# A gated feed-forward layer behind pooled attention: the last 3072 tokens by seven products of half-size blocks, with combined weights streamed from DRAM

## The chip, the cores and the metric

The kernel runs on one core of a Trainium2 chip. Its engines have a queue each and work in parallel: TensorE (PE in the profile; PEld is its weight load), VectorE (DVE), ScalarE (ACT), GpSimd (POOL), and SyncE (SP), whose queue issues the transfers here. Each queue is worked through in order. The metric is the device time of one execution in microseconds, the median of several runs.

## The reference

Only the arithmetic matters; S is 576, so K and V are averaged over 8 rows to 72 rows.

```python
k_p = k.reshape(B, H, Sp, 8, D).mean(axis=3)        # B = 8 images, H = 8 heads, D = 64
v_p = v.reshape(B, H, Sp, 8, D).mean(axis=3)
scores = (q @ k_p.transpose(0, 1, 3, 2)) / sqrt(D)
attn = exp(scores - max(scores)); attn = attn / (sum(attn) + 1e-9)
x = (attn @ v_p).transpose(0, 2, 1, 3).reshape(4608, 512)
h = x @ w_in                                         # 512 -> 2048
g = h * clip(h + 3, 0, 6) / 6
out = g @ w_out                                      # 2048 -> 512
```

## The kernel before

The 4608 tokens are worked through in blocks, `BLOCKS = [512, 256, 384] + [512] * 6 + [384]`. For a block the kernel has x in transposed form (4 chunks of 128 model dimensions by the block's tokens), as a sum of two reduced-precision parts, `xhi` and `xlo`; the weights lie in SBUF in two such parts as well (`w_in_hi`, `w_in_lo`, `w_out_hi`, `w_out_lo`, made once at the start, in the pool `const`). A product of two such matrices takes three matmuls: high by high, high by low, low by high.

A block runs 16 steps, one for each group f of 128 of the 2048 hidden columns. `Step.h` (matmuls on L782) computes h for f: 4 chunks by 3 matmuls, as wide as the block has tokens. `relu` (ACT, L790) and `gate` (DVE, L794) make g; `hi` (ACT, L798) and `lo` (DVE, L802) split it. `Step.out` (L812), two steps later, adds g for f into one PSUM bank per 128 tokens: 3 matmuls of 512 columns for each. After the last f the banks are scaled (ACT, L818) and stored (L819).

Attention for the next block runs between these matmuls. `Paced` hands its steps out, one or a few at each `slot()`. A block of 384 tokens has three tiles of 128 tokens with two head groups each; for each of these six, `scores` does the products (L412), the maximum (DVE, L416), four exponentials on ACT (L420; each is an ACTIVATE and a read of its sum), the reciprocal (DVE, L436 and L437) and the division on POOL (L448, L454); then transposes on PE (L518, L520), their copies on ACT and DVE, and the products with V (L583), copied into `x` by ACT (L585). `side_steps` load and pool K and V of the next image. `split_x` (L561, L562) splits x before a block's first h.

The start, up to the fourth step of block 1, has an order written out by hand (`ORDER`); after it a scheduler sets each queue's order when the program is built, from data dependences and an estimate of times. On the chip the queues then keep that order.

## Time and profile before

| | |
|---|---|
| median of 3 runs | 921.58 us (921.29 to 921.69) |
| span of the profiled execution, first to last instruction | 920.7 us |
| PE busy in it | 908.4 us, 99% |
| DVE, ACT, POOL busy | 456.5, 461.5, 81.1 us |
| granted TensorE clock | 1.000 |
| transfers | 57.19 MB, mean 62 GB/s |

The profile gives no time of the profiled execution apart from its span; the median of the runs lies 0.9 us above the span, for what surrounds the first and the last instruction. Rows of instructions give line, engine, operation, tiles (out<-in), shapes, count, then busy time and mean ns of one. In the chain of waits, one row is start, duration and what ran. In the timeline, "SPq" is a DMA issue by SP.

### The profile page before, as it was taken

To read this page: it belongs to the slowest core of one execution; us is meant where nothing else is said; L and a number is where in the kernel's file an instruction comes from. 1 tells how busy PE (TensorE), PEld (TensorE's weight loads), DVE (VectorE), ACT (ScalarE), POOL (GpSimd) and SP (SyncE) were. 2 spreads that over 40 slices of the span, in tenths; PEclk is the share of its full clock that TensorE was granted. 3 is DMA by queue.
4 is the path that set the end of the run, shared out by engine and by line. 5 is a ranking of instruction groups with operands and counts; after the bars stand their busy time and mean duration, and the time that the engine had idled before them with its cause. 6 is when DMAs were issued, how large, how long until landed. Compare 5 with 4: busy or idle time off the path is not lost.

```text
span 920.7 us, 12711 instructions
## 1 busy us (share of the span) xinstructions
PE 908.4 (99%) x4568; PEld 777.6 (84%) x4568; DVE 456.5 (50%) x916; ACT 461.5 (50%) x1340; POOL 81.1 (9%) x167
## 2 busy tenths in 40 slices
PE   7899999999999999999999999999999999999998
PEld 6788889999888888888888888888888888888997
DVE  6999855475356333824356326633356224332322
ACT  5998665465355434633456335633545344333322
POOL 4100001021000100101011101110101001000000
PEclk9999999999999999999999999999999999999999
DMA  9970203050031002300042004200210000000100
GB/s 295 391 262 0 92 12 121 1 167 18 1 113 59 24 1 79 106 12 6 0 143 59 12 1 136 60 12 1 91 40 25 1 34 24 1 0 1 47 1 35
DMA packets 41935, 57.19 MB, mean 62 GB/s; under 512 B 7568, under 2 KB 23696, under 8 KB 41872
## 3 DMA queue, kind: packets, MB, share of 16 engines
q1 hardware_dynamic: 41728, 56.37, 19.0%
q8 instruction: 36, 0.59, 0.3%
q14 instruction: 27, 0.22, 0.1%
q10 hardware_dynamic: 144, 0.00, 0.0%
HBM read 46.93 MB, written 9.44 MB: 61 GB/s over the span
## 4 chain that ended last, share of the span: by engine, by line
PE 96%; DMA 3%; DVE 1%; issue 0%; SPq 0%; ACT 0%; ACTq 0%; DVEq 0%
PE pso L812 43%; PE psh L782 43%; PE psa L583 4%; PE psa L412 4%; PE psa L518 2%; DMA raw<-w_in_l 1%; DMA raw<-w_out_l 1%; DMA stage<-k_l 1%; PE psa L520 0%; SPq L257 0%; ACT stage L420 0%; DVE u L689 0%; DVE u L700 0%; DVE stage L448 0%; DVE a L510 0%
## 5 line engine op out<-in xcount | busy, mean ns | idle before, releaser
L782 PE MATMUL psh<-xhi,w 128*128 128x512 f32 (+2 forms) x1288 | 401.9, 372 | 0.0
L812 PE MATMUL pso<-w,ghi 128*128 128x512 f32 (+1 forms) x1184 | 367.0, 391 | 0.0
L782 PEld LDWEIGHTS psh<-xhi,w 128*128 128x128 f32 x1288 | 237.7, 188 | 36.1 <-issue 0.4
L812 PEld LDWEIGHTS pso<-w,ghi 128*128 128x128 f32 x1184 | 214.2, 188 | 36.0
L782 PE MATMUL psh<-xlo,w 128*128 128x512 f32 (+2 forms) x644 | 237.4, 369 | 0.0
L794 DVE SCALAR_TENSOR_TENSOR g<-g,psh 128x512 f32<-128x512 f32 (+2 forms) x161 | 101.3, 629 | 271.5 <-ACT g L790 270.3
L812 PE MATMUL pso<-w,glo 128*128 128x512 f32 (+1 forms) x592 | 225.9, 386 | 0.0
L790 ACT ACTIVATE g<-psh,small 128x512 f32<-128x512 f32 (+2 forms) x161 | 103.7, 644 | 208.7 <-PE psh L782 192.3
L782 PEld LDWEIGHTS psh<-xlo,w 128*128 128x128 f32 x644 | 121.2, 188 | 18.1
L802 DVE TENSOR_TENSOR glo<-g,ghi 128x512 fp32r<-128x512 f32 (+2 forms) x161 | 102.3, 635 | 62.0 <-ACT ghi L798 60.1
L812 PEld LDWEIGHTS pso<-w,glo 128*128 128x128 f32 x592 | 111.1, 188 | 21.7
L798 ACT CAST ghi<-g 128x512 fp32r<-128x512 f32 (+2 forms) x161 | 92.9, 577 | 70.0 <-DVE g L794 67.4
L420 ACT ACTIVATE e<-psa,mx 128x72 f32<-128x72 f32 x256 | 78.6, 322 | 50.6 <-DVE mx L416 49.9
L448 POOL TENSOR_TENSOR a<-e,sm 128x256 f32<-128x256 f32 x60 | 40.5, 675 | 513.5 <-PE pso L812 180.3
L420 ACT ACTIVATION_READ_ACCUMULATOR e<-psa,mx 128x1 f32 x256 | 52.9, 207 | 0.0
L416 DVE TENSOR_REDUCE mx<-psa 128x4 f32<-128x288 f32 x72 | 32.3, 453 | 29.5 <-PE psa L412 29.0
L412 PEld LDWEIGHTS psa<-kbd,qt 128*128 128x128 f32 x288 | 43.1, 189 | 4.2
L412 PE MATMUL psa<-kbd,qt 128*128 128x144 f32 x288 | 45.5, 285 | 0.0
L585 ACT COPY x<-psa 128x192 f32<-128x192 f32 (+7 forms) x60 | 22.9, 386 | 32.6 <-PE psa L583 32.4
L332 DVE TENSOR_REDUCE vsum<-vst 128x64 f32<-128x512 f32 (+1 forms) x36 | 37.7, 1065 | 2.6 <-DMA vst<-v_l 2.0
L436 DVE TENSOR_SCALAR sm<-sm 128x4 f32<-128x4 f32 x72 | 12.6, 178 | 48.9 <-ACT e L420 45.7
L529 ACT CAST ahi<-psa 128x256 fp32r<-128x256 f32 (+1 forms) x70 | 24.5, 352 | 18.7 <-PE psa L518 9.8
(93 smaller groups left out, 630.7 us busy)
## 6 DMA issues: line engine op xcount, KB each, us to landing
out<-o SPq DMA_DIRECT2D x35, 256.0 KB, 2.3
raw<-w_in_l SPq DMA_DIRECT2D x16, 512.0 KB, 8.5
raw<-w_out_l SPq DMA_DIRECT2D x16, 512.0 KB, 9.2
kst<-k_l SPq DMA_DIRECT2D x28, 288.0 KB, 3.0
qt<-q_l SPq DMA_DIRECT2D x28, 256.0 KB, 3.3
vst<-v_l SPq DMA_DIRECT2D x24, 256.0 KB, 3.1
vst<-vr_l SPq DMA_DIRECT2D x36, 64.0 KB, 1.9
stage<-k_l SPq DMA_DIRECT2D x4, 288.0 KB, 4.1
```

Source lines behind the costliest of these rows:

```text
L332: nc.vector.tensor_reduce(out=vs[:n, p], in_=st[:n, : POOL * D].rearrange("p (o d) -> p d o", o=POOL), axis=AX.X, op=ALU.add)
L412: nc.tensor.matmul(to, qt[:, p, :], kbds[b % 2][:, p, :], start=r == 0, stop=r == last)
L416: nc.vector.tensor_reduce(out=self.mx, in_=self.ps, axis=AX.X, op=ALU.max, negate=True)
L420: nc.scalar.activation(self.e[:, h], self.ps[:, h], AF.Exp, bias=self.mx[:, h : h + 1], accum_out=self.sm[:, h : h + 1])
L448: engine.tensor_tensor(out=self.a[:, : 4 * D].rearrange("p (h s) -> p h s", h=4), in0=e[:, :, :D], in1=sm[:, :, None].broadcast_to([P, 4, D]),
L583: nc.tensor.matmul(ps, l, r, start=n == 0, stop=n == len(mms) - 1)
L782: nc.tensor.matmul(self.ps, l[f][:, c, :], r[:, c, :], start=c == 0 and i == 0, stop=c == NCC - 1 and i == 2)
L790: nc.scalar.activation(self.g, self.ps, AF.Relu, bias=half, scale=1.0 / (6.0 * WSCALE))
L794: nc.vector.scalar_tensor_tensor(out=g, in0=g, scalar=1.0, in1=self.ps, op0=ALU.min, op1=ALU.mult)
L798: nc.scalar.copy(self.ghi, self.g)
L802: nc.vector.tensor_tensor(out=self.glo, in0=self.g, in1=self.ghi.bitcast(F32), op=ALU.subtract)
L812: nc.tensor.matmul(pos, l, r[:, cols], start=f == 0 and i == 0, stop=f == NF - 1 and i == 2)
```

## The change

The first 1536 tokens are four blocks of 512, 256, 384 and 384 and run as before (`PLAIN = 4`). The other 3072 form four super blocks of two 384-token halves. In a super block both layers are computed by a 2x2 split of each matrix product, with the seven products of the Strassen-Winograd scheme in place of eight: halves of the tokens, of the contraction, and of the output columns.

For h, the hidden columns are taken in 8 pairs of f; each pair has seven products (`N1`, 56 in all) of a combined weight block (128 hidden columns by 256 model dimensions) and a combined x block (256 dimensions by 384 tokens). Each is 2 chunks by 3 matmuls of 384 columns. `PERIOD` interleaves pairs so that a product has its PSUM bank free. Sums between products are kept by ACT copies (`keep`) and DVE adds (`plus`); four gates per pair leave g in four quadrants, `g_of[i]`, that stay in SBUF. For out, `N2` runs the seven kinds in the order `KINDS`, each over the 8 pairs: a g quadrant or a sum of quadrants (made on POOL) is split by `split_op` on ACT and DVE, and multiplied by a combined w_out block of 256 columns: 3 token tiles by 3 matmuls of 256 columns. The seven combined x blocks (`x_ops`) are made on POOL, ACT and DVE during the last 16 products of the super block before.

The combined weights do not fit in SBUF. They are made during the plain blocks 2 and 3, one `sums_of` call at each of the 32 steps: six POOL operations in a buffer `wq`, a high part on ACT in `wh`, a low part on DVE in place, and eight DMA writes of 64 KB to DRAM; blocks that need no sum are copied from the weights. `wq` and `wh` have two buffers each. In a super block `next_w` loads them back, two products to a 512 KB chunk, into a ring of 6 chunks (`ws`), five ahead; each super block reads all 56 chunks.

SBUF is shared out anew: the pools `early` and `const` are released behind block 3, and `late`, with everything of the super blocks, lies on the same addresses; `x1` lies over the weights of f = 14 and 13. The attention of the next blocks is spread over N1 and over the first 40 products of N2; half of block 3's attention moves into block 1. The last tile's split in two banks at the end of the program is gone.

The diff, cut to its core:

```diff
-BLOCKS = [512, 256, 384] + [512] * 6 + [384]
+BLOCKS = [512, 256, 384, 384] + [384] * 8
+PLAIN = 4
+HALF = 384
...
+PERIOD = ((1, 0), (2, 0), (7, 1), (5, 0), (6, 0), (4, 1), (3, 0))
+KINDS = (1, 2, 6, 5, 7, 3, 4)
+RAW_LEFT = {1: (0, 0), 2: (0, 1), 4: (1, 1)}
+RAW_RIGHT = {1: (0, 0), 2: (1, 0), 3: (1, 1)}
+CHUNK, NSTREAM, AHEAD, NOP, NC, NRO = 2, 6, 5, 4, 4, 4
 WSCALE = 2.0**8
+GSCALE = WSCALE**-2
...
     psum = ctx.enter_context(tc.tile_pool(name="psum", bufs=1, space=PSUM))
+    const = tc.alloc_tile_pool(name="const", bufs=1, reuse_waits="tile")
+    early = [tc.alloc_tile_pool(name="early0", bufs=1, reuse_waits="tile")]
...
+    NPR = NF // 2
+    N1 = [(1, i, o) for t in range(NPR + 1) for o, d in PERIOD for i in [t - d] if 0 <= i < NPR]
+    N2 = [(2, i, o) for o in KINDS for i in range(NPR)]
+    stream = N1 + N2
+    place_of = {x: n for n, x in enumerate(stream)}
...
+    def dram_of(kind, i, o):
+        n = place_of[kind, i, o]
+        return w_dram[n // CHUNK][:, n % CHUNK]
...
+    def sums_of(kind, i, h):
+        half = slice(h * P, (h + 1) * P)
+        qs = early[-1].tile([P, 4, P], F32, name="wq", bufs=2)
+        pairs = [w_of[2 * i + r, kind - 1].bitcast(F32).rearrange("p m (q c) -> p m q c", q=2) for r in range(2)]
+        for r, w in enumerate(pairs):
+            nc.gpsimd.tensor_tensor(
+                out=qs[:, 2 * r : 2 * r + 2], in0=w[:, 0, :, half], in1=w[:, 1, :, half], op=ALU.add
+            )
+        mixed = combine_left(qs, nc.gpsimd) if kind == 1 else combine_right(qs, nc.gpsimd)
+        hi = early[-1].tile([P, 4, P], F32, name="wh", bufs=2)
+        nc.scalar.copy(hi.bitcast(F32R), qs)
+        nc.vector.tensor_tensor(out=qs.bitcast(F32R), in0=qs, in1=hi, op=ALU.subtract)
+        for o, q in mixed.items():
+            for m, t in enumerate((hi, qs)):
+                nc.sync.dma_start(dram_of(kind, i, o)[:, m, half], t[:, q])
+        if h:
+            return
+        for o, (r, q) in (RAW_LEFT if kind == 1 else RAW_RIGHT).items():
+            nc.sync.dma_start(dram_of(kind, i, o), pairs[r][:, :, q])
+    def combine_left(q, engine):
+        def op(to, a, b, how):
+            engine.tensor_tensor(out=q[:, to], in0=q[:, a], in1=q[:, b], op=how)
+        op(0, 0, 2, ALU.subtract)
+        op(2, 2, 3, ALU.add)
+        op(3, 3, 0, ALU.subtract)
+        op(1, 1, 3, ALU.subtract)
+        return {7: 0, 3: 1, 5: 2, 6: 3}
...
+    def next_w(x):
...
+        n, loaded = w_stream
+        while n * CHUNK <= place_of[x] + CHUNK * AHEAD and n < len(w_dram):
+            loaded[n] = late.tile([P, CHUNK, 2, 2 * P], F32R, name="ws", bufs=NSTREAM)
+            nc.sync.dma_start(loaded[n].bitcast(F32), w_dram[n])
+            n += 1
+        w_stream[0] = n
+        at = place_of[x]
+        return loaded[at // CHUNK][:, at % CHUNK]
+    def split_op(t, src):
+        nc.scalar.copy(t[:, 0], src)
+        nc.vector.tensor_tensor(out=t[:, 1], in0=src, in1=t[:, 0].bitcast(F32), op=ALU.subtract)
...
+    def x_ops(j, steps, now=False):
...
+        a, b = (x_tile(i, "x", F32) for i in (j, j + 1))
+        b11, b21, b12, b22 = a[:, :2], a[:, 2:], b[:, :2], b[:, 2:]
+        def split(o, src):
+            def make(c):
+                if c == 0:
+                    x_op[o] = late.tile([P, 2, 2, HALF], F32R, name=f"x{o}")
+                split_op(x_op[o][:, :, c], src[:, c])
+            return [lambda c=c: make(c) for c in range(2)]
...
+        early_ones = split(1, b11) + split(2, b21)
+        late_ones = (
+            mix(None, b22, b12, ALU.subtract)
+            + split(3, b22)
+            + mix(b12, b12, b11, ALU.subtract)
+            + mix(b11, b11, None, ALU.add)
+            + [lambda c=c, o=o: split(o, mid[0])[c]() for o in (7,) for c in range(2)]
+            + split(6, b11)
+            + mix(b21, b21, b11, ALU.subtract)
+            + split(5, b12)
+            + split(4, b21)
+        )
...
+    def super_block(j, first_att, second_att):
...
+        def bank(names, i, n=HALF):
+            return psum.tile([P, DM], F32, name="psx", tag=names[i % len(names)])[:, :n]
+        def gate(src, q):
...
+            nc.scalar.activation(r, src, AF.Relu, bias=half_low, scale=GSCALE / (6.0 * WSCALE))
+            nc.vector.scalar_tensor_tensor(
+                out=g_of[i][:, k], in0=r, scalar=GSCALE, in1=src, op0=ALU.min, op1=ALU.mult
+            )
...
+        def plus(q, ps, kept):
+            i, k = q
+            nc.vector.tensor_tensor(out=g_of[i][:, k], in0=ps, in1=kept, op=ALU.add)
+            gate(g_of[i][:, k], q)
+        def keep(c, ps):
+            nc.scalar.copy(c, ps)
+            return c
...
+        for x in N1:
+            _, i, o = x
+            if o == 1:
+                g_of[i] = late.tile([P, 4, HALF], F32, name=f"g{i}")
+                c = [late.tile([P, 2, HALF], F32, name="c", bufs=NC) for _ in range(2)]
+                chain[i] = [bank(["h0", "h1", "o0"], i), bank(["o1"], i), bank(["o2"], i), c, {}]
+            X, Y, Z, c, kept = chain[i]
+            ps = {1: X, 2: Z, 3: Y, 4: X, 5: Y, 6: X, 7: X}[o]
+            w, t = next_w(x), ops[o]
+            paced.slot()
...
+            if o == 1:
+                kept[1] = keep(c[0][:, 0], X)
+            elif o == 2:
+                plus((i, 0), Z, kept[1])
+            elif o == 5:
+                kept[5] = keep(c[1][:, 0], Y)
+            elif o == 6:
+                kept[2] = keep(c[0][:, 1], X)
+            elif o == 3:
+                plus((i, 2), Y, kept[2])
+            elif o == 7:
+                plus((i, 3), X, kept[5])
+            elif o == 4:
+                gate(X, (i, 1))
+                g = g_of[i]
+                mix_of[i] = late.tile([P, HALF], F32, name=f"e{i}")
+                nc.gpsimd.tensor_tensor(out=g[:, 2], in0=g[:, 2], in1=g[:, 3], op=ALU.add)
+                nc.gpsimd.tensor_tensor(out=mix_of[i], in0=g[:, 2], in1=g[:, 0], op=ALU.subtract)
...
+        paced = Paced(second_att, len(N2) - n_tail)
+        X2, Y2 = ([bank(names, p, 2 * P) for p in range(NT2)] for names in (["o0", "o3", "h0"], ["h1", "o1", "o2"]))
...
+        def result(t, m, ps, kept):
+            o = late.tile([P, 2 * P], F32, name="o", tag="ro", bufs=NRO)
+            if kept is None:
+                nc.scalar.copy(o, ps)
+            else:
+                nc.vector.tensor_tensor(out=o, in0=ps, in1=kept, op=ALU.add)
+            store(t, m, o)
...
+        for n, x in enumerate(N2):
+            _, i, o = x
...
+            t = late.tile([P, 2, HALF], F32R, name="op", bufs=NOP)
+            split_op(t, src)
+            if o == 1:
+                nc.gpsimd.tensor_tensor(out=g[:, 0], in0=g[:, 3], in1=mix_of[i], op=ALU.subtract)
+            elif o == 2:
+                nc.gpsimd.tensor_tensor(out=g[:, 1], in0=g[:, 1], in1=mix_of[i], op=ALU.subtract)
+            w = next_w(x)
+            if n < len(N2) - n_tail:
+                paced.slot()
+            elif ahead:
+                ahead.pop(0)()
...
+            if n == len(N2) - n_tail - 1:
+                paced.upto(len(paced.steps))
+                if j + 2 < len(BLOCKS):
+                    ahead = first_x + later_x
+            if i < NPR - 1:
+                continue
+            if o in (1, 5, 6):
+                c = late.tile([P, 2, HALF], F32, name="c", bufs=NC).rearrange("p a b -> p (a b)")
+                kept[o] = [keep(c[:, p * 2 * P : (p + 1) * 2 * P], ps) for p, ps in enumerate(X2 if o != 5 else Y2)]
...
-            if steps[0].blk.j == 1 and u == 3:
+                if side:
+                    side.pop(0)()
+            if j == 1 and u == 3:
                 window.append(len(traced))
+                paced.add_more()
...
             if u == len(steps) - 1:
-                paced.upto(len(attention))
-                if attention:
-                    split_x(steps[0].blk.j + 1)
-            if u >= len(steps) and steps[0].blk.j == len(BLOCKS) - 1:
-                continue
+                paced.upto(len(paced.steps))
+                if j + 1 < PLAIN and j != 1:
+                    split_x(j + 1)
             if u >= lag:
                 steps[u - lag].out(slot)
...
+        assert not side
+        if j == 1:
+            early.pop().release()
+            early.append(tc.alloc_tile_pool(name="early1", bufs=1, reuse_waits="tile"))
+            split_x(j + 1)
...
+    third = att_steps(3)
+    cut = len(third) // 2
+    for j, mine, more, side in (
+        (1, att_steps(2), third[:cut], ()),
+        (2, third[cut:] + att_steps(4), (), side_weights[:NF]),
+        (3, att_steps(5), (), side_weights[NF:]),
+    ):
         blk = Block(j, ["o0", "o1", "o2", "o3"])
-        run([Step(blk, f, 0, blk.nt) for f in range(NF)], 2, att_steps(j + 1))
+        run([Step(blk, f, 0, blk.nt) for f in range(NF)], 2, mine, more=more, side=side)
+    early.pop().release()
+    const.release()
+    late = ctx.enter_context(tc.tile_pool(name="late", bufs=1, reuse_waits="tile"))
+    supers = range(PLAIN, len(BLOCKS), 2)
+    x_ops(PLAIN, [], now=True)
+    for j in supers:
+        last = j == supers[-1]
+        super_block(j, [] if last else att_steps(j + 2), [] if last else att_steps(j + 3))
```

Three places in the order of the queues. First ACT, at the end of block 1 (tokens 512 to 767), toward block 2. Before, the splits of x for block 2 (`xhi`) stand ahead of eight exponentials (`e`) and the evictions of block 1's sums (`o<-pso`):

```order
L790 ACTIVATE g<-psh,small 128x256
L561 CAST xhi<-x 128x384 x4
L798 CAST ghi<-g 128x256
L420 ACTIVATE e,sm<-psa,mx 128x72 x8
L818 ACTIVATE o<-pso 128x512 x2
L790 ACTIVATE g<-psh,small 128x384
```

After, at the same place:

```order
L809 ACTIVATE g<-psh,small 128x256
L438 ACTIVATE e,sm<-psa,mx 128x72 x4
L817 CAST ghi<-g 128x256
L438 ACTIVATE e,sm<-psa,mx 128x72 x8
L836 ACTIVATE o<-pso 128x512 x2
L585 CAST xhi<-x 128x384 x4
```

The splits of x that block 2's first h needs now stand behind the exponentials and evictions. Next ACT after the change at the end of block 3, from its evictions toward `x_4321`, the first combined x block (`x1`) of the first super block:

```order
L836 ACTIVATE o<-pso 128x512 x3
L609 COPY x<-psa 128x384
L438 ACTIVATE e,sm<-psa,mx 128x72 x12
L900 CAST wh<-wq 128x512
L438 ACTIVATE e,sm<-psa,mx 128x72 x4
L547 CAST ahi<-psa 128x2x128
L438 ACTIVATE e,sm<-psa,mx 128x72 x2
L900 CAST wh<-wq 128x512
L438 ACTIVATE e,sm<-psa,mx 128x72 x2
L547 CAST ahi<-psa 128x2x128
L558 CAST arem<-psa 64x128
L438 ACTIVATE e,sm<-psa,mx 128x72 x2
```

Behind these stand two more exponentials, a copy of each kind (`arem`, `ahi`), and then the splits of `x1`. All 24 exponentials of a block's attention and the high parts of the last two weight sums are between the end of the plain blocks and the first operand of the first super block. Last SP after the change at the same point, where the writes of the last weight sum (`wd<-wh`, `wd<-wq`) stand ahead of the first chunk of streamed weights (`ws<-wd_86`):

```order
L904 DMA wd_125<-wq 128x128
L904 DMA wd_129<-wq 128x128
L904 DMA wd_141<-wh 128x128
L904 DMA wd_141<-wq 128x128
L904 DMA wd_133<-wh 128x128
L904 DMA wd_133<-wq 128x128
L246 DMA vst<-v_l 128x512
L251 DMA vst<-vr_l 32x512
L944 DMA ws<-wd_86 128x1024
L944 DMA ws<-wd_87 128x1024
```

Before, there was no such stream: SP had loads of q, k and v and stores alone here.

## Prediction

> **What bounds the kernel now.** I read the busy shares of the page first, then the chain of waits, then a table by stage.

> ```profile
> PE 908.4 (99%) x4568; PEld 777.6 (84%) x4568; DVE 456.5 (50%) x916; ACT 461.5 (50%) x1340; POOL 81.1 (9%) x167
> PEclk9999999999999999999999999999999999999999
> PE 96%; DMA 3%; DVE 1%; issue 0%; SPq 0%; ACT 0%; ACTq 0%; DVEq 0%
> PE pso L812 43%; PE psh L782 43%; PE psa L583 4%; PE psa L412 4%; PE psa L518 2%; DMA raw<-w_in_l 1%; DMA raw<-w_out_l 1%; DMA stage<-k_l 1%; PE psa L520 0%; SPq L257 0%; ACT stage L420 0%; DVE u L689 0%; DVE u L700 0%; DVE stage L448 0%; D
> 0.00:38.00 38.00, 28.99 (x188) 26.16 (x189) 28.31 (x65) 27.44 (x94) 12.67 (x29) 1.00 1.00 332
> 270.00:860.00 590.00, 590.00 (x2811) 494.31 (x2810) 261.90 (x533) 266.40 (x807) 51.21 (x102) 1.00 0.13 40
> 860.00:920.70 60.70, 57.44 (x329) 53.31 (x327) 14.97 (x28) 15.82 (x29) 0.00 (x0) 1.00 0.04 14
> ```

> PE works for 99% of the span at a granted clock of 1.000, which I take for the changed kernel too. In the long middle it has no gap at all (590.00 of 590.00 us), while DVE works 261.90, ACT 266.40 and POOL 51.21 us, and DMA moves 40 GB/s. The 9.0 us in which PE waits lie in the first 38 us, which the change leaves almost as they are, and the 3.3 us of the last row. So PE's matmuls are the time: fewer or narrower matmuls shorten it directly, unless they let PE wait. What a matmul costs stands in the chain, by width:

> ```profile
> 271.50 2.72 PE pso L812 x12
> 862.87 2.11 PE psh L782 x12
> 145.31 1.42 PE psh L782 x12
> 497.51 2.75 PE psh L782 x12
> ```

> From 2.72, 2.11 and 1.42 us for twelve, one of 512 columns takes 0.227, of 384 0.176, of 256 0.118 us. Most rows of the chain with twelve of 512 read as the one at 497.51, 0.229; I use 0.228, 0.1755 and 0.119. Check: 3012 of 512 columns, 384 of 384 and 312 of 256 in the lines 782 and 812 (my count of the program: the small ones are 216 and 96) give 791 us; two times 43% of 920.7 is 792.

> **Term 1, the products: −50 us.** Removed are six blocks of 512 tokens, each 16 steps of 12 matmuls for h and 12 for out, all 512 wide: 2304 × 0.228 = 525.3 us. Added are four super blocks of 56 products: 1344 matmuls of 384 columns × 0.1755 = 235.9, and 2016 of 256 × 0.119 = 239.9, together 475.8; the net is −49.5. Attention's matmuls stay the same columns in all, the block of 384 at the end became the plain block 3.

> ```profile
> L782 PEld LDWEIGHTS psh<-xhi,w 128*128 128x128 f32 x1288 | 237.7, 188 | 36.1 <-issue 0.4
> ```

> Every matmul has its own weight load, 188 ns by this row, and in N2 the matmuls are shorter than that. Yet in the row at 145.31 twelve of 256 columns, each with its load, take 119 ns apiece: the loads are hidden there. [...]

> **What takes from it.** In the plain blocks all is as wide as before or narrower, and four new duties arise. For them these rows:

> ```profile
> L420 ACT ACTIVATE e<-psa,mx 128x72 f32<-128x72 f32 x256 | 78.6, 322 | 50.6 <-DVE mx L416 49.9
> L420 ACT ACTIVATION_READ_ACCUMULATOR e<-psa,mx 128x1 f32 x256 | 52.9, 207 | 0.0
> L585 ACT COPY x<-psa 128x384 f32<-128x384 f32 x12 | 5.7, 479 | 5.0 <-PE psa L583 4.9
> L723 ACT CAST w<-u 128x512 fp32r<-128x512 f32 x4 | 2.5, 626 | 1.1 <-DVE u L700 1.1
> L818 ACT ACTIVATE o<-pso 128x512 f32<-128x512 f32 x35 | 18.7, 601 | 16.3 <-PE pso L812 16.2
> L529 ACT CAST ahi<-psa 128x256 fp32r<-128x256 f32 x56 | 20.9, 373 | 16.8 <-PE psa L518 9.5 <-PE psa L520 7.3
> L728 DVE TENSOR_TENSOR w<-u,w 128x512 fp32r<-128x512 f32 x4 | 2.7, 684 | 2.2 <-ACT w L723 2.1
> L448 POOL TENSOR_TENSOR a<-e,sm 128x256 f32<-128x256 f32 x60 | 40.5, 675 | 513.5 <-PE pso L812 180.3 <-DVE sm L437 157.8 <-PE psa L520 94.2
> L454 POOL TENSOR_TENSOR ar<-e,sm 128x64 f32<-128x64 f32 x60 | 21.3, 357 | 106.1 <-DVE sm L437 61.9 <-ACT g L790 29.7 <-ACT kbd L222 9.1
> 263.84 1.34 SPq L819 DMA_DIRECT2D out<-o  x3
> raw<-w_in_l SPq DMA_DIRECT2D x16, 512.0 KB, 8.5
> out<-o SPq DMA_DIRECT2D x2, 128.0 KB, 1.7
> vst<-vr_l SPq DMA_DIRECT2D x36, 64.0 KB, 1.9
> ```

> **Term 2, from block 3 to the first super block: +17 us.** By the second order place, ACT goes through these once the last `out` of block 3 is near its end: 3 evictions (3 × 0.60 = 1.8), one copy (0.48), 24 exponentials with their reads (24 × 0.529 = 12.7), two high parts of weights (1.25), four smaller casts (0.37 or less each by the `ahi` row, about 1.5), then the first half of `x1` (0.5): 18.2 us. The first weights come by SP, whose order has the last sum's eight writes ahead: the second high part ends about 13.4 us in (2.3, 18 exponentials 9.5, one `ahi` 0.4, two high parts 1.25), its low part on DVE takes 0.7, the writes that follow it 2.7 (six × 0.45, from 1.34 us for three issues), two loads 0.9, the first chunk's issue 0.45, its landing about 3 (between 1.7 us for 128 KB and 8.5 us for 512 KB at full load): 21 us. PE has in that time only attention:

> ```profile
> 123.55 0.49 PE psa L412 x4
> 158.13 0.22 PE psa L518 x2
> 176.60 0.70 PE psa L583 x4
> ```

> One product with V, six scores and twelve transposes are 0.70 + 6 × 0.49 + 12 × 0.11 = 5.0 us. So PE stands for 21 − 5 = 16, with the sum's other waits 17. Bounds: 13 if the weights don't come last, 26 if the chunk lands at 8.5 us.

> **Term 3, from block 1 to 2: +4 us.** By the first order place the x splits stand behind eight exponentials (4.2 us) and two evictions (1.2), where they stood ahead; PE has the last two `out` to do meanwhile. Bounds 0 and 5.4.

> **Term 4, the weight sums in blocks 2 and 3: +8 us.** A buffer pair `wq`/`wh` serves every second step. One turn: POOL's two adds of 256 columns (0.675 each) and four of 128 (0.463, on the line between the two POOL rows), 3.2 us; the high part 0.63, the low part 0.68, six to eight issues 2.7 to 3.6, the last landing 1.8 (64 KB by the `vst` row, 1.9): 9.0 to 9.9. Two steps of PE take 2 × (12 × 0.1755 + 9 × 0.228 + 0.5 of attention) = 9.3. So there is no slack. If a turn is late, POOL is late, `wh` is late, and behind it on ACT stands `relu`, which PE's next h waits for. POOL also waits for DVE:

> ```profile
> 373.08 1.15 POOL L448 TENSOR_TENSOR a<-e,sm 128x256 f32<-128x256 f32 x1 [10.93 <-DVE sm L436]
> 373.10 0.66 DVE L802 TENSOR_TENSOR glo<-g,ghi 128x512 fp32r<-128x512 f32 x1
> 425.90 0.61 POOL L448 TENSOR_TENSOR a<-e,sm 128x256 f32<-128x256 f32 x1 [3.48 <-PE psa L520]
> ```

> The same POOL operation took 1.15 us where it began beside a DVE subtraction with both inputs in SBUF (373.08 and 373.10), and 0.61 where none ran. [...] A step has two such DVE operations (`lo` and the low part), so a turn may grow by up to 2.2 us. Bounds: 0 where every turn fits, 16 turns × 2.2 = 35 us where each is 11.5 us long. I take 8: a third of the turns late by 1.5.

> **Term 5, DVE in the first N1: +8 us.** Seven pairs of N1 are PE's 49 products of 6 × 0.1755 = 1.05, 51.6 us, with 5.7 of attention 57.3. DVE does in the same stretch of the order:

> ```profile
> L794 DVE SCALAR_TENSOR_TENSOR g<-g,psh 128x384 f32<-128x384 f32 x32 | 17.7, 552 | 59.5 <-ACT g L790 59.4
> L802 DVE TENSOR_TENSOR glo<-g,ghi 128x384 fp32r<-128x384 f32 x32 | 17.8, 556 | 13.7 <-ACT ghi L798 13.7
> L332 DVE TENSOR_REDUCE vsum<-vst 128x64 f32<-128x512 f32 x24 | 25.0, 1066 | 2.1 <-DMA vst<-v_l 2.0
> L214 DVE TENSOR_REDUCE ksum<-kst 128x72 f32<-128x576 f32 x28 | 20.9, 746 | 5.8 <-DMA kst<-k_l 4.9 <-ACT kbd L222 0.7
> L416 DVE TENSOR_REDUCE mx<-psa 128x4 f32<-128x288 f32 x72 | 32.3, 453 | 29.5 <-PE psa L412 29.0
> ```

> 27 gates (14.9), 19 `plus` and 10 x splits (29 × 0.556 = 16.1), 11 V sums (11.7), 6 K sums (4.5), 6 maxima (2.7), smaller ones 8.7: 58.6 us. One bank set is freed by `plus`, so a late DVE stops PE. 1.3 us are over at once, and DVE, which takes its queue in order, will have gaps of its own: I take 8. Bounds 1 and 20 (the 11.7 us of V sums and the smaller 8.7 all in the way). The next N1 have 37, 33 and 28 us of DVE for 55, 52 and 48 of PE: no cost.

> **Term 6, the other seams: +6 us.** At the end of each super block, DVE has 16 operand splits and 14 x splits (30 × 0.556 = 16.7) for PE's 16 products of 1.07 = 17.1; three such ends and the three changes N1 to N2, about 1 us each. The end keeps its 3.3 us: a sum and a store. Bounds 0 and 15.

> **Sum:** −50 + 17 + 4 + 8 + 8 + 6 = −7: a span of 913.7. The profiled span is 920.7, the median 0.9 above it: **914.6 us**.

> The streamed weights I cost at nothing. One super block reads 29.4 MB in 56 chunks while PE needs 119 us: 512 KB per 2.1 us, 250 GB/s. Before, it never had to be so for long, but:

> ```profile
> 20.00:30.00 10.00, 8.90 (x58) 7.61 (x57) 9.33 (x24) 9.31 (x37) 1.21 (x2) 1.00 1.04 398
> GB/s 295 391 262 0 92 12 121 1 167 18 1 113 59 24 1 79 106 12 6 0 143 59 12 1 136 60 12 1 91 40 25 1 34 24 1 0 1 47 1 35
> ```

> 398 GB/s were moved over ten microseconds with the DMA share at 1.04. Five chunks ahead are 10.5 us, a little over the 8.5 us of the `raw` row, which was landing under that full load.

> **Rivals.**
> (a) *The covers hold*: terms 4 to 6 fall to nothing, 2 and 3 stay: 920.7 − 49.5 + 21 + 0.9 = 893. Its range is 884 to 905, from the lower ends of terms 2 and 3 to half of 4 to 6. For it: DVE 50% and ACT 50% busy. Against: no slack in term 4.
> (b) *The ring of weight sums paces blocks 2 and 3* (ends on the other side). Each turn of two steps takes 11.5 us in place of 9.3, from POOL waiting for DVE's two-input operations. 16 turns × 2.2 = 35 in place of 8: 941.6; range 924 to 955. From a turn of 10.4 us (16 × 1.05 = 16.8 in place of 8) it makes the kernel slower than before; 955 has the upper end of term 2 beside it. For it: 9.0 to 9.9 without any blocking, and the 1.15 us row. Against: the order places the sums in ACT's and DVE's gaps, and a sum may run ahead by one buffer.
> (c) *The stream is late.* If chunks came at 200 GB/s (the start's slices moved 262 to 391), 117 MB would take 587 us in place of 476: +111, about 1026.
> (d) *Loads show in N2*, by the row of 188 ns: 2016 × 69 ns = +139, about 1054. [...]

> **How the numbers follow.** Forecast, 905 to 919.7: 0.38. (a) 0.18. Within 0.2% (919.7 to 923.4, as much as a measurement of this kernel can tell from no change): 0.06. (b) 0.34. (c) 0.03. (d) 0.01. Faster: 0.38 + 0.18 = 0.56; same 0.06; slower 0.34 + 0.03 + 0.01 = 0.38. The range leaves out the fast end of (a), the far end of (b), and (c) and (d): 886 to 948. The forecast's own range is 905 to 919.7.

> **What would show it.** Term 1: rows of six matmuls in 1.05 us for N1, of nine in 1.07 us for N2. Term 2: one gap of PE of some 16 us before the first super block, ended by `ws` or `x1`. Term 4: in blocks 2 and 3, PE waiting for `relu`, ACT before it for POOL's `wq`, POOL for the write that empties `wq`; turns of 9.3 or more. Term 5: PE in the first N1 waiting for a `plus` on DVE, none in the later ones. (b) is right if PE's idle time in blocks 2 and 3 passes 20 us. (c): PE waiting for `ws` in the middle of a super block. I would be wrong first of all if PE's idle time came in many small waits inside the N1 and N2 that no term here has.

## The result, and the profile after

The changed kernel takes 950.09 us, median of 4 runs (946.85 to 953.9), against 921.63 us before: a ratio of 1.031, 95% interval 1.028 to 1.034. It is slower, 35 us over the forecast and 2 us past the end of its range.

The page of the kernel after, its busy shares, the granted clock in 40 slices, and the chain of waits by engine:

```profile
span 952.0 us, 17078 instructions
PE 891.8 (94%) x5576; PEld 835.6 (88%) x5576; DVE 679.6 (71%) x1271; ACT 579.4 (61%) x1684; POOL 376.9 (40%) x504
PEclk9999999999899995799999999999999999999999
PE 53%; DVE 19%; DMA 10%; POOL 6%; SPq 4%; issue 4%; ACT 4%; POOLq 0%; ACTq 0%; DVEq 0%
```

PE worked 99% of the span before; now it is idle for 952.0 − 891.8 = 60.2 us, where it was 12.3. The chain was PE for 96%; now it passes through DVE (19%), DMA, POOL and ACT as well. And the clock row, all 9s before, dips: in slice 16 to a half. A table by stretch, of the six in which the granted clock was 0.5:

```profile
254.60:261.40 6.80, 5.95 (x18) 5.12 (x19) 6.28 (x14) 3.94 (x15) 5.12 (x9) 0.50 0.38 98
360.50:394.60 34.10, 19.26 (x59) 15.34 (x60) 25.63 (x49) 19.82 (x79) 20.05 (x30) 0.50 0.74 241
445.80:449.20 3.40, 3.40 (x12) 3.40 (x11) 2.84 (x8) 3.23 (x15) 0.00 (x0) 0.50 1.00 363
490.20:493.60 3.40, 3.40 (x18) 3.40 (x17) 3.34 (x8) 1.62 (x5) 0.50 (x1) 0.50 0.56 195
688.10:691.50 3.40, 3.09 (x11) 2.69 (x10) 1.37 (x5) 3.21 (x13) 0.91 (x2) 0.51 0.48 158
811.00:814.40 3.40, 3.40 (x17) 3.40 (x18) 3.40 (x8) 1.18 (x3) 0.00 (x0) 0.50 0.69 235
sum 54.50, PE 38.50 PEld 33.35 DVE 42.85 ACT 33.01 POOL 26.57; mean PE 6.42 PEld 5.56 DVE 7.14 ACT 5.50 POOL 4.43
```

PE was busy for 38.5 of these 54.5 us and did in them the work of half that time: 19.3 us are lost. The span's growth of 31.3 us can so be split in four. Products: −49.5. Idle time: 60.2 − 12.3 = +47.9. Half clock: +19.3. The rest, 13.6, is what is left over; I put it down to waits too short to be seen as idle (a PE instruction's end is modelled), which no row shows by itself. The waits that I had forecast come to 43, and 47.9 of idle time were found: it is the clock and this rest that are on top. The profiled execution is the slowest of the four (953.9 us): its stages add up to some 4 us more than those of the median.

Where it is lost, by stage. For each, the time beyond PE's work at full speed (number of matmuls of each kind by their mean spacing in the kernel before between 130 and 840 us, attention's among them, worked out from the start times in the traces; 174.5 ns for 384 columns and 119.3 for 256). I call this time the excess. The work is 900.2 us before and 844.7 after. Seam is the time from block 3's last product to the first of the super blocks; N1 and N2 are of the first super block.

| us beyond full-speed work | start, block 1 | blocks 2, 3 | seam | first N1 | first N2 | other three, end | all |
|---|---|---|---|---|---|---|---|
| before (blocks 4 to 9 as one) | 18.5 | 0.3 | – | – | – | 1.7 | 20.5 |
| after | 19.7 | 14.6 | 22.3 | 13.8 | 11.4 | 25.5 | 107.3 |

How the excess divides depends on how attention's short matmuls are counted. With each width at its plain mean spacing the work after is 840.0 us, and the columns shift by up to 5 us (the start 14.5, blocks 2 and 3 18.1, the first N1 15.3, the last 30.3); the seam and the first N2 stay, and the differences between runs stay within 0.3 us.

The forecast of the products held. Rows of the chain of waits in N1 and N2 (start, duration, count):

```profile
778.64 1.08 PE psx L1109 x9
830.67 46.14 PE psx L1038 x264
900.23 47.88 PE psx L1109 x388
```

264 matmuls of 384 columns in 46.14 us are 0.175 each, a product's nine of 256 in 1.08 us 0.120, 388 in a row 0.123. The forecast had 0.1755 and 0.119.

```profile
DMA packets 127448, 204.30 MB, mean 215 GB/s; under 512 B 16384, under 2 KB 83456, under 8 KB 127360
ws<-wd SPq DMA_DIRECT2D x224, 512.0 KB, 4.4
PE psx L1038 <- DMA ws<-wd: 2.7, 2, 2.3
PE psx L1109 <- DMA ws<-wd: 0.5, 1, 0.5
```

The streamed weights (median landing 4.4 us for 512 KB) made PE wait three times, 3.2 us in all, 2.3 of them at the seam. That cost was rightly put at about nothing.

**The seam.** Rows of the timeline from there, POOL, ACT, PE, SP, DVE, in order of time (in brackets the engine's idle time before, and what ended it):

```profile
355.15 1.43 POOL L895 TENSOR_TENSOR wq<-w 128x256 f32<-128x256 f32 x2 [2.18 <-DMA wd<-wq]
358.74 0.62 ACT L900 CAST wh<-wq 128x512 fp32r<-128x512 f32 x1 [4.36 <-POOL wq L924]
361.25 2.56 PE L430 MATMUL psa<-kbd,qt 128*128 128x144 f32 x8 [4.13 <-ACT x L609]
372.03 0.61 ACT L900 CAST wh<-wq 128x512 fp32r<-128x512 f32 x1
377.58 0.42 SPq L944 DMA_DIRECT2D ws<-wd  x1
378.35 2.57 ACT L951 CAST x<-x 128x384 fp32r<-128x384 f32 x6
378.89 2.68 DVE L952 TENSOR_TENSOR x<-x,x 128x384 fp32r<-128x384 f32 x2
382.15 3.54 PE L1038 MATMUL psx<-x,ws 128*128 128x384 f32 x10 [2.33 <-DMA ws<-wd]
```

POOL waits 2.18 us for the write that empties `wq`; ACT waits 4.36 us for POOL's sum (`wh`), and behind it on ACT stand the evictions and the copy of x that PE waits 4.13 us for. The last high part is made at 372.03, 15 us after block 3's end (357); behind its writes SP issues the first chunk at 377.58, and PE begins at 382.15, by the landing of `ws`. Its ten matmuls of 384 columns then take 3.54 us, 0.354 each: half clock. The 24 exponentials that I had counted into this gap stood there too, between the evictions (the last begins at 360.23) and the first split of `x1` on ACT at 378.35, with 6.9 us in which ACT waited. Its low part on DVE was ready at 381.57, 0.6 us before PE began: two chains, the weights and `x1`, ended almost together here.

**N2.** Rows of DVE, POOL and PE shortly before 811 us, in the third super block:

```profile
803.18 2.04 POOL L975 TENSOR_TENSOR x<-x 128x768 f32<-128x768 f32 x1
803.44 2.20 DVE L952 TENSOR_TENSOR op<-g,op 128x384 fp32r<-128x384 f32 x1
805.30 2.04 POOL L975 TENSOR_TENSOR x<-x,mid 128x768 f32<-128x768 f32 x1
806.01 1.74 DVE L952 TENSOR_TENSOR op<-g,op 128x384 fp32r<-128x384 f32 x1
810.87 1.55 PE L1109 MATMUL psx<-ws,op 128*128 128x256 f32 x6 [1.60 <-DVE op L952]
L952 DVE TENSOR_TENSOR op<-g,op 128x384 fp32r<-128x384 f32 x192 | 139.3, 744 | 41.0 <-ACT op L951 40.2
PE psx L1109 <- DVE op L952: 10.4, 18, 1.6
```

While POOL makes a sum for the combined x blocks (2.04 us), a split on DVE takes 2.20 and 1.74 us instead of 0.55; then PE waits 1.60 us for the next split, and at 811.0 the clock halves (the table above). Over all, these splits take 0.744 us in the mean, and PE waits 10.4 us for them.

### The profile page after: what moved, and what is told of

Same layout as the page of the kernel before. It is cut to its first block, busy times and chain, and to the rows that moved or that the text cites. A ratio compares the mean times of both kernels' runs of the same rounds, so it can differ in the third digit from the quotient of the medians.

```text
span 952.0 us, 17078 instructions
## 1 busy us (share of the span) xinstructions
PE 891.8 (94%) x5576; PEld 835.6 (88%) x5576; DVE 679.6 (71%) x1271; ACT 579.4 (61%) x1684; POOL 376.9 (40%) x504
## 4 chain that ended last, share of the span: by engine, by line
PE 53%; DVE 19%; DMA 10%; POOL 6%; SPq 4%; issue 4%; ACT 4%; POOLq 0%; ACTq 0%; DVEq 0%
PE psx L1038 20%; PE psx L1109 17%; PE psh L801 7%; PE pso L831 6%; DVE op L952 5%; DMA wd<-wq 3%; POOL wq L895 3%; DMA kst<-k_l 2%; SPq L904 2%; DVE x L952 2%; PE psa L607 2%; DVE vsum L350 2%; POOL wq L924 2%; DMA vst<-vr_l 2%; PE psa L430 2%
## 5 line engine op out<-in xcount | busy, mean ns | idle before, releaser
L1109 PE MATMUL psx<-ws,op 128*128 128x256 f32 x2016 | 265.7, 288 | 11.6 <-DVE op L952 10.4
L1109 PEld LDWEIGHTS psx<-ws,op 128*128 128x128 f32 x2016 | 252.6, 193 | 19.2 <-DVE op L952 17.1
L1038 PE MATMUL psx<-x,ws 128*128 128x384 f32 x1344 | 258.0, 344 | 10.6 <-DMA ws<-wd 2.7
L1038 PEld LDWEIGHTS psx<-x,ws 128*128 128x128 f32 x1344 | 236.8, 192 | 15.0 <-ACT c L1023 2.9
L952 DVE TENSOR_TENSOR op<-g,op 128x384 fp32r<-128x384 f32 x192 | 139.3, 744 | 41.0 <-ACT op L951 40.2
L801 PE MATMUL psh<-xhi,w 128*128 128x384 f32 (+2 forms) x520 | 146.1, 340 | 2.6 <-DVE g L813 1.7
L951 ACT CAST op<-g 128x384 fp32r<-128x384 f32 x192 | 96.6, 517 | 73.5 <-PE psx L1109 69.1
L831 PE MATMUL pso<-w,ghi 128*128 128x512 f32 x384 | 122.7, 402 | 0.0
L801 PEld LDWEIGHTS psh<-xhi,w 128*128 128x128 f32 x520 | 93.8, 189 | 10.7 <-DVE g L813 2.7
L1062 POOL TENSOR_TENSOR g<-g 128x384 f32<-128x384 f32 x32 | 33.2, 1039 | 139.4 <-DVE g L1013 139.4
L831 PEld LDWEIGHTS pso<-w,ghi 128*128 128x128 f32 x384 | 70.1, 191 | 10.8
L1023 ACT COPY c<-psx 128x384 f32<-128x384 f32 (+1 forms) x132 | 54.5, 453 | 26.3 <-PE psx L1038 24.1
L895 POOL TENSOR_TENSOR wq<-w 128x256 f32<-128x256 f32 x64 | 50.7, 814 | 31.3 <-DMA wd<-wq 23.8
L430 PE MATMUL psa<-kbd,qt 128*128 128x144 f32 x288 | 50.2, 303 | 10.4 <-ACT x L609 4.1
## 6 DMA issues: line engine op xcount, KB each, us to landing
ws<-wd SPq DMA_DIRECT2D x224, 512.0 KB, 4.4
raw<-w_in_l SPq DMA_DIRECT2D x16, 512.0 KB, 9.3
raw<-w_out_l SPq DMA_DIRECT2D x16, 512.0 KB, 9.2
```

Of the source, the lines that this page charges most:

```text
L430: nc.tensor.matmul(to, qt[:, p, :], kbds[b % 2][:, p, :], start=r == 0, stop=r == last)
L801: nc.tensor.matmul(self.ps, l[f][:, c, :], r[:, c, :], start=c == 0 and i == 0, stop=c == NCC - 1 and i == 2)
L831: nc.tensor.matmul(pos, l, r, start=f == 0 and i == 0, stop=f == NF - 1 and i == 2)
L895: nc.gpsimd.tensor_tensor(out=qs[:, 2 * r : 2 * r + 2], in0=w[:, 0, :, half], in1=w[:, 1, :, half], op=ALU.add)
L951: nc.scalar.copy(t[:, 0], src)
L952: nc.vector.tensor_tensor(out=t[:, 1], in0=src, in1=t[:, 0].bitcast(F32), op=ALU.subtract)
```

## The experiments

Three theories, each with a rival. **R**: the ring of weight sums is late, and the seam waits for its end. **L** (the lock): where POOL's sums and DVE's operations with two inputs in SBUF run together, they hold each other up (POOL 1.15 us in place of 0.61 in the kernel before, a split up to 2.20 in place of 0.55 in the kernel after), and PE waits for the splits. **C**: behind a long enough wait of PE the clock halves for a while. Later **B**: DVE's load bounds the first super block. All changes are against the kernel after unless it says otherwise; times are medians.

**The clock by itself.** In the kernel before, at twelve places, in outline:

```diff
+    first = matmul(start, ident, ident)      # behind all earlier matmuls
+    nc.scalar.copy(d, start)
+    for _ in range(n): nc.scalar.copy(d, d)  # n = 1 to 20
+    second = matmul(..., ident, d)           # all later matmuls behind it
```

> The kernel before, with PE stopped on purpose at twelve places in its blocks 3 to 8: a small matmul waits for a chain of 2 to 21 ACT copies, some 0.3 to 5 us; nothing else is changed. Theory C (the granted clock halves behind a wait of PE that is long enough, and stays so for a whole number of 3.41 us): waits up to about 1.5 us are followed by none, those of 2.5 us and more by a stretch at half clock in which matmuls of 512 columns stand 0.45 us apart in place of 0.23, and each such stretch costs about 1.7 us beyond the wait. Rival: the half-clock stretches in the changed kernel come from something else (the weight stream, DMA load); then all twelve leave the clock at 1.000 and the time is longer by the waits alone.

993.87 us (one run), PE idle for 53.8 us in place of 12.3. The timeline shows how long PE waited, and a table by stretch the clock behind it:

```profile
400.18 0.49 PE L1057 MATMUL psa<-gap,ident 128*128 128x128 f32 x2 [1.34 <-ACT gap L1056]
507.94 0.49 PE L1057 MATMUL psa<-gap,ident 128*128 128x128 f32 x2 [2.44 <-ACT gap L1056]
...
400.20:403.60 3.40, 3.40 (x18) 2.92 (x19) 0.87 (x3) 0.92 (x3) 0.00 (x0) 1.00 0.37 88
508.85:512.25 3.40, 3.40 (x11) 2.61 (x10) 2.20 (x4) 0.83 (x2) 0.61 (x1) 0.50 0.49 129
512.30:515.70 3.40, 3.40 (x18) 2.83 (x18) 2.94 (x8) 2.69 (x9) 0.00 (x0) 1.00 0.26 101
```

Behind the wait of 1.34 us the clock stays at 1.00 and 18 matmuls start in 3.4 us; behind 2.44 us it is 0.50 and 11 start; 3.4 us later it is back. Ten of the twelve places were followed by one to three such stretches of 3.41 us, the two of 1.34 us by none. 54.6 us lay at half clock, the matmuls in them took some 21 us more than at full clock. C holds; nothing was added there but the wait and the small operations that make it. Two shorter waits near each other did it too: in the kernel after 1.02 and 0.65 us within the same 3.41 us, ahead of the stretch at 490.2.

The way back asks for more. A table of the last two windows of 3.41 us in the kernel after's long stretch:

```profile
387.80:391.20 3.40, 1.51 (x5) 1.54 (x6) 3.37 (x7) 1.93 (x6) 0.66 (x1) 0.50 1.07 330
391.20:394.60 3.40, 3.40 (x12) 3.40 (x11) 3.28 (x9) 2.15 (x6) 0.00 (x0) 0.50 0.12 44
```

The stretch ended behind its first window in which PE had no gap (3.40 of 3.40 us busy, in the second row). In the eight windows ahead of these two, PE was idle for 0.86 to 2.74 us by the trace, in the first of these rows for 1.9, and each was followed by another at half clock. At full clock even the wait of 1.34 us above changed nothing; 0.86 us within a window was enough to keep a clock low that was low already. So the seam's stretch lasted 34 us.

**The weight sums left out.**

```diff
...
-        mixed = combine_left(qs, nc.gpsimd) if kind == 1 else combine_right(qs, nc.gpsimd)
...
-        nc.scalar.copy(hi.bitcast(F32R), qs)
-        nc.vector.tensor_tensor(out=qs.bitcast(F32R), in0=qs, in1=hi, op=ALU.subtract)
...
-                nc.sync.dma_start(dram_of(kind, i, o)[:, m, half], t[:, q])
+                nc.sync.dma_start(dram_of(kind, i, o)[:, m, half], pairs[q // 2][:, m, q % 2, half])
```

> Leaves out the sums of the weights: the same 256 writes of 64 KB are there, but they take blocks of the weights as they are, so no POOL, ACT or DVE work and no two-buffer ring stands in blocks 2 and 3. Theory R (the ring of weight sums is late and paces blocks 2 and 3 and, by its last writes, the start of the first super block): most of the 23.5 us over full-speed work between block 3 and the first super block goes, and some 10 of those in blocks 2 and 3 and at the first N1; 900 to 912 us. Rival S (the seam itself, with attention and the splits of x behind one another): the seam keeps 15 us or more, over 930 us.

934.57 us (931.97 to 935.64): a third of what theory R expected. The seam did vanish, as a table by stretch shows, the kernel after first, then this one (second number: PE's busy time of 26.00 us):

```profile
356.00:382.00 26.00, 10.92 (x40) 7.81 (x38) 14.29 (x32) 16.39 (x70) 18.17 (x33) 0.59 0.67 205
...
356.00:382.00 26.00, 22.40 (x107) 20.02 (x106) 23.51 (x44) 19.80 (x79) 13.10 (x15) 0.80 0.79 271
```

The seam's excess fell from 22.3 to 2.0 us. But the first N2 rose from 11.4 to 17.2: attention that had stood in the seam now stood behind it. R is right about the seam and wrong about the sum. The run does not part the sums from the exponentials, though: with the sums gone the scheduler put the splits of `x1` right behind the evictions, with no exponential between:

```profile
360.70 2.63 ACT L943 CAST x<-x 128x384 fp32r<-128x384 f32 x6
```

**The super blocks' sums on DVE.** The sums of x (L975) and of g (L1062, L1063, L1098, L1100):

```diff
-                nc.gpsimd.tensor_tensor(out=dst, in0=p_, in1=q_, op=how)
+                nc.vector.tensor_tensor(out=dst, in0=p_, in1=q_, op=how)
...
-                nc.gpsimd.tensor_tensor(out=g[:, 2], in0=g[:, 2], in1=g[:, 3], op=ALU.add)
+                nc.vector.tensor_tensor(out=g[:, 2], in0=g[:, 2], in1=g[:, 3], op=ALU.add)
```

> All sums of the super blocks (of x for the combined blocks, of g) move from POOL to DVE. Theory L (POOL's long sums shut out DVE's two-input operations, a split then takes up to 2.2 us and PE waits for it): the mean of the 224 operand splits on DVE falls from 0.74 to below 0.62 us, PE's waits for them from 10 to below 4 us, and with the half-clock stretches that these waits bring the time falls by 8 to 20 us, to 930 to 942. Rival D (DVE has no room): DVE's busy time rises by 40 us or more, PE waits for it elsewhere, 948 us or more.

931.92 us (931.22 to 935.0). From the groups and the waits of PE:

```profile
L952 DVE TENSOR_TENSOR op<-g,op 128x384 fp32r<-128x384 f32 x192 | 104.9, 558 | 45.5 <-ACT op L951 45.0
PE psx L1109 <- DVE op L952: 4.1, 4, 1.2
```

The same split takes 0.558 in place of 0.744 us, PE waits 4.1 in place of 10.4, and the excess of the first N2 falls from 11.4 to 6.8 and that of the other super blocks from 25.5 to 12.6. No half-clock stretch is left between the first N2 and the program's end, where the kernel after has three. L holds (PE's waits are a hair over the 4 that it named), and its rival does not: DVE's busy time rose by 8 us only (679.6 to 687.6), since the 224 splits alone lost 41. The sums themselves also became shorter, 0.554 in place of 1.039 us for the first of g (L1062); how much of the 18 us is the lock, and how much the shorter way to an operand, was not separated. The lock by itself can be read in the start and end times of the kernel after: a split of g (`op<-g`) that began while a POOL sum ran took 1.125 us in the mean (64 of them), one with no POOL sum beside it 0.554 (120). All of the 64 that took over 0.9 us ended 0.41 to 0.42 us behind the end of that sum. `plus`, which reads one input from PSUM, took 0.555 and 0.554 us in these two cases.

**Two writes a sum.** The combined weights lie in DRAM by pairs, so that one write takes all four high parts and one all low parts; a chunk is read by two loads.

```diff
-        for o, q in mixed.items():
-            for m, t in enumerate((hi, qs)):
-                nc.sync.dma_start(dram_of(kind, i, o)[:, m, half], t[:, q])
+        for m, t in enumerate((hi, qs)):
+            nc.sync.dma_start(w_dram[kind, i][:, 3:, m, half], t)
```

> A sum's eight writes of 64 KB become two of 256 KB (the combined weights lie in another order in DRAM, and a chunk is read by two loads). Theory R: the turn of the ring loses about six issues of 0.43 us, 11.6 us becomes about 9.0, and the last sums end some 20 us earlier against the end of block 3: 918 to 932 us. Rival S: blocks and seam stay as they are, 945 us or more; the rival that POOL's own 3.9 us a sum pace it gives a turn near 10 and 936 to 944 us.

936.71 us (935.01 to 940.66), between the two. From the starts of the first and the last of the 32 high parts in the traces, two sums take 11.5 us in the kernel after and 10.9 here, where 9.0 was expected; POOL still waits for the writes, more often than before:

```profile
POOL wq L895 <- DMA wd<-wq: 23.8, 15, 3.1
...
POOL wq L896 <- DMA wd<-wq: 29.5, 19, 3.7
```

The turn did not fall by the six issues saved, though the last sums ended 10 us earlier and the seam fell to 12.5 us. The time lies in the range of the rival that POOL's own work paces the sums, though a turn of 10.9 is not its "near 10"; what took the place of the issues is not shown.

**Both together**, the edits of the last two.

> Two writes a sum and the super blocks' sums on DVE, together. Theories R and L are about different stretches, so the gains add: 950 - 18 - 13 = 919, 915 to 924 us. Rival: both only lengthen DVE's and ACT's queues at the seam, and the second gives nothing more: 930 us or more.

922.66 us (921.13 to 924.49); 1.001 of before (1.000 to 1.002). The gains added nearly as expected. It is the first version that comes within 0.2% of the kernel before; it is not faster.

**Keeping PE at work in the seam.**

```diff
+    for _ in range(NWARM):                # NWARM = 100; behind block 3's last product
+        nc.tensor.matmul(warm[:, :P], ident, ident, start=True, stop=True)
```

> The changed kernel with 100 small matmuls on an unused bank between block 3 and the first super block, so that PE works there (a part of its order there moves with them: attention stands behind the first products). Theory C: the half-clock stretch of 34 us at the seam shrinks to under 10 and the first N1's matmuls stand 0.175 us apart; the wait for the weights stays, so 938 to 946 us. Rival: the clock plays no part, the first N1 waits for its operands anyway: 948 us or more.

949.08 us (947.19 to 952.74): no gain that the runs can tell (the profiled execution was 6.6 us shorter, 945.4 us, within their spread). The stretch of 34 us at half clock is gone, and N1 starts at full clock:

```profile
PEclk9999999999999999999999999999999999999999
380.82 3.44 PE L1039 MATMUL psx<-x,ws 128*128 128x384 f32 x16 [1.67 <-DMA ws<-wd]
```

The first N1's excess fell from 13.8 to 5.6 us. What it gained went: PE's first product is still released by `ws` (380.82 for 382.15), attention moved behind it (first N2 11.4 to 12.7, with 3.6 us more work in it). So C's mechanism is there, and most of its price at the seam did not come back: there the half clock fell together with a wait that stayed. The time lies in the range of the rival.

**More of the sums off POOL.** Both together, and every second weight sum on DVE:

```diff
+        eng = nc.vector if h else nc.gpsimd
...
-        mixed = combine_left(qs, nc.gpsimd) if kind == 1 else combine_right(qs, nc.gpsimd)
+        mixed = combine_left(qs, eng) if kind == 1 else combine_right(qs, eng)
```

> As both together, and every second weight sum is made on DVE in place of POOL. Theory R (POOL's 3.9 us a sum is then the longest part of the ring's turn): the last sums end before block 3 does, and the first N1 follows block 3 within 5 us: 903 to 915 us. Rival D (DVE's share in blocks 2 and 3 is full with it): blocks 2 and 3 lose what the seam gains, 918 us or more.

923.9 us (921.39 to 924.82). The seam went to 0.9 us, as R has it, here from the same stretch as above:

```profile
356.00:382.00 26.00, 22.56 (x119) 19.68 (x118) 18.93 (x40) 18.98 (x65) 3.77 (x7) 1.00 0.66 225
```

but blocks 2 and 3 went from 15.3 (both together) to 21.8, the first super block from 19.9 to 21.5, and the time is in rival D's range. Every fourth:

```diff
-        eng = nc.vector if h else nc.gpsimd
+        eng = nc.vector if h and i % 2 else nc.gpsimd
```

> As both together, and every fourth weight sum on DVE in place of POOL (where every second gave the seam's 13 us back to blocks 2 and 3). Theory R: the last sums end with block 3, the seam keeps under 5 us beyond full-speed work, and blocks 2 and 3 lose less than with every second: 910 to 918 us. Rival D: what the seam gains is lost again in blocks 2 and 3 and the first super block, whose DVE, ACT and attention are as full as before: 919 to 925 us.

930.24 us (929.86 to 932.26), seam 1.0, blocks 2 and 3 21.0, first super block 28.8: outside both ranges and slower than both its neighbours (922.66 and 923.9). What the seam gave is lost in the places that rival D names, but more than that is lost. The order of the queues comes out differently with each edit; how much of the 6 to 8 us is its doing was not separated. The same with all of block 3's attention in block 1:

```diff
-    cut = len(third) // 2
+    cut = len(third)
```

> As the kernel with every fourth sum on DVE, and all of block 3's attention runs in block 1, where before it was half. Rival D's test: if blocks 2 to the first super block are short of room for attention beside the sums, moving some of it ahead gains there what block 1 can take, 5 to 10 us less than the kernel with every fourth sum; if not, the same within 3 us, or slower since attention of later blocks moves up into the seam.

926.84 us (925.87 to 929.59): 3.4 us less, between the two expectations. Blocks 2 and 3 fell to 16.5, and the seam rose to 12.3, as the second said.

**DVE's load.** Both together, N1's two sums of g (L1062, L1063 in the kernel after) back on POOL, of which the first is shown:

```diff
-                nc.vector.tensor_tensor(out=g[:, 2], in0=g[:, 2], in1=g[:, 3], op=ALU.add)
+                nc.gpsimd.tensor_tensor(out=g[:, 2], in0=g[:, 2], in1=g[:, 3], op=ALU.add)
```

> As both together, but the two sums of g for each pair in N1 go back to POOL; those of N2 and of x stay on DVE. Theory B (DVE, at 63 of 71 us in the first N1 and 69 of 77 in the first N2, is what bounds the first super block): 64 sums of 0.55 us less on DVE, 9 us in each N1, take 3 to 8 us off the first super block's waits; 914 to 920 us. Theory L alone (each sum on POOL shuts out DVE's two-input work for about a microsecond): N1 loses what DVE gains, 921 to 930 us.

924.06 us (921.42 to 926.22, 12 runs). The first N2 went from 11.6 to 8.3, the third super block's N1 from −0.3 to 6.0: nothing won, and the time is in the range of theory L alone. It is no test of B in the first N1: DVE was to lose 9 us there and lost 2.0 (62.66 to 60.70), and N1's excess did not fall. And with the sums of K and V cut to one row for the images from the fifth on (V shown, K alike):

```diff
+    def short_v(b, t):
+        return t[:, :D].rearrange("p (o d) -> p d o", o=1) if b >= 4 else t.rearrange("p (o d) -> p d o", o=POOL)
...
-            out=vs[:n, p], in_=st[:n, : POOL * D].rearrange("p (o d) -> p d o", o=POOL), axis=AX.X, op=ALU.add
+            out=vs[:n, p], in_=short_v(b, st[:n, : POOL * D]), axis=AX.X, op=ALU.add
```

> As both together, but the sums of K and V over 8 rows for the images of the super blocks take one row in place of 8 (that part of attention is left out), so DVE loses some 40 us of work, most of it in the first two super blocks. Theory B (DVE, 89% busy in the first super block, bounds it once lock and ring are gone): PE's time beyond full-speed work in the first super block falls from 20 to under 10 us, and the time to 908 to 915 us. Rival (the waits there come from the order of the queues and from DMA, not from DVE's load): 919 us or more.

919.4 us (914.23 to 923.47, 10 runs), 0.997 of before (0.995 to 0.999): 0.4 us inside the range of the rival, and not in B's. First N1 and first N2, both together and then this one (third busy time: DVE):

```profile
373.30:443.90 70.60, 65.50 (x371) 62.81 (x371) 62.66 (x133) 46.47 (x141) 6.37 (x13) 0.98 0.84 269
443.90:521.20 77.30, 71.24 (x549) 69.38 (x548) 69.09 (x149) 49.81 (x142) 4.61 (x8) 0.96 0.82 261
...
373.80:437.60 63.80, 62.91 (x362) 62.42 (x362) 53.60 (x130) 43.73 (x130) 6.95 (x13) 0.97 0.88 288
437.60:513.60 76.00, 71.72 (x555) 70.44 (x555) 60.69 (x148) 51.20 (x152) 4.28 (x8) 0.96 0.87 278
```

DVE fell from 62.66 to 53.60 us in N1, and N1 took 63.8 in place of 70.6 us, its excess 8.3 to 2.4. In N2 DVE fell by 8.4 us and the excess only from 11.6 to 9.5. Together that is 19.9 to 11.9, where B expected under 10. In N1 the run speaks for B; for the whole super block it does not, and what holds N2 is not settled.

**No weight sums and sums on DVE**, the first two experiments in one:

> No weight sums (left out as in the run without them) and the super blocks' sums on DVE: what the change would take if the combined weights cost no engine anything. Theories R and L add: 934.6 - 18 = 916, and 910 to 918 us. If the gain of 49 us in products is held up by the weight sums and the lock alone, under 895 us; if the first super block's DVE bounds whatever is taken away ahead of it, 920 us or more.

917.96 us (916.82 to 919.36), 0.995 of before (0.994 to 0.997). That is the range for R and L adding up, and not the one under 895. So even with the weights' sums free and the lock gone, 49.5 us of products bring 4 us. The excess by stage, of all runs that matter here:

| us beyond full-speed work | start, block 1 | blocks 2, 3 | seam | first N1 | first N2 | other three, end | all |
|---|---|---|---|---|---|---|---|
| after | 19.7 | 14.6 | 22.3 | 13.8 | 11.4 | 25.5 | 107.3 |
| no weight sums | 22.3 | 13.5 | 2.0 | 10.9 | 17.2 | 22.6 | 88.4 |
| sums on DVE | 19.3 | 13.2 | 22.1 | 10.9 | 6.8 | 12.6 | 84.8 |
| both together | 20.5 | 15.3 | 13.0 | 8.3 | 11.6 | 9.3 | 78.0 |
| every second sum on DVE too | 20.4 | 21.8 | 0.9 | 8.9 | 12.6 | 12.1 | 76.9 |
| no weight sums, sums on DVE | 21.7 | 12.3 | 2.1 | 6.7 | 14.1 | 15.8 | 72.9 |

About 76 is the break-even: the 20.5 of before and the 55.5 of full-speed work saved. That saving is 49.5 in the forecast's spacings and about 62 if every matmul of 512 columns counts its mean spacing before, 0.233, where attention's short ones stand among them; counted otherwise, the rows and the break-even shift together.

## Why the prediction was wrong, point by point

The step that failed most is term 6: it put the stretches behind the first N1 at 6 us, and they cost 36.9. Of the 38 us between the forecast span of 913.7 and the profiled 952.0, some 29 lie there (36.9 less the 6 of the term and the 1.7 of before); the first N1 and the seam add 5 to 6 each, blocks 2 and 3 about 2, and the work was some 6 smaller than forecast. The half clock, put at nothing, is spread over these places.

- **Term 1, the products (−49.5)**: right, by the rows at 830.67 and 900.23. With it the rival that weight loads show in N2 is refuted: 0.120 us a matmul beside a load of 0.193 us. So is the rival of the late stream.
- **The clock**: "which I take for the changed kernel too" was the sentence that failed first. In these runs it held only where PE's waits were short (in the kernel before 1.75 us at most in a window of 3.41 us), and I forecast some 40 us of waits. Half speed took 19.3 us, of which 9.6 in the seam's stretch; keeping PE at work there brought 1.0 us in the medians. The kernel with gaps shows it alone: 1.00 behind a wait of 1.34 us, 0.50 behind one of 2.44. In the kernel after the seam's first wait was 4.13 us; ahead of the other five of the six stretches, waits of 1.7 to 2.6 us in all within 3.41 us were enough.
- **Term 6, the other seams (+6)**: the term that was mis-sized most. It stood for all of N2 and the later N1; measured are 11.4 in the first N2 and 25.5 in the rest. I had quoted the pair of rows in which POOL's operation took 1.15 us beside DVE's of 0.66, and 0.61 without, and used them for the weight sums alone; the super blocks have POOL sums of 1 to 2 us beside the splits that PE waits for. About 5 of these 36.9 us are half clock (the stretches at 490.2, 688.1 and 811.0). The sums on DVE took 17.5 away; what makes up the rest is open. That the later N1 cost nothing held for two of three (1.4 and −0.2 us; 4.3 in the third super block).
- **Term 2, the seam (+17)**: 22.3 in the gap, ended by `ws` as said. Of its two chains I had the one through the exponentials about right: `x1` was ready 0.6 us before PE began. The other, the last sums, ended 15 us late, and that I did not forecast. Which of the two sets the seam alone is not shown, since the run without weight sums moved the exponentials too; with every second sum on DVE it closed as well (0.9), and there also no exponential stood ahead of `x1`.
- **Terms 3 and 4 (+4, +8)**: 14.6 together. The size is near, which is luck in good part: a turn was put at 9.0 to 9.9 us and is 11.5, and of PE's 9.8 us of idle time in blocks 2 and 3 the waits that I had named are small (1.7 us for the gate behind `relu`, 1.3 for `xhi` and `xlo`), beside 5.6 for attention's own `alo` and `a`. The turn is rival (b)'s 11.5, and its mechanism, POOL and ACT waiting in the ring, is there; but the sums fell behind the blocks, so that its price was paid at the seam. By its own sign, over 20 us of idle time in blocks 2 and 3, (b) fails. Its forecast of 941.6 was the nearest and its range holds the result, though most of the miss lies in N2 and the later super blocks, of which it says nothing.
- **Term 5, the first N1 (+8)**: 13.8, some 6 of it by half clock (8.9 us of PE's busy time in its first 12 us and 3.4 at 445.8, at half speed). The wait for a `plus` that I had named is 0.4 us; the longest are 2.3 us for `alo` and 2.0 for a gate, both on DVE. That DVE's load is behind the rest is made likely by the short sums of K and V, in the version with both edits (8.3 to 2.4).
- Not seen at all: that the terms are not independent. What one wait gives up, attention takes elsewhere. Without weight sums the seam gave 20 us back and the time 15.5. I take this to be why no run came near the −49.5; no run shows it alone.

Open: what holds the first N2 at 7 to 18 us in every version, and whether an order of the queues exists that keeps the seam and blocks 2 and 3 short at the same time. No order was written out by hand to try it.
